# Attention with scores turned both ways: the key-major units take PV with V as weights, and their softmax totals come from Pool, a DMA turn and VectorE

## The chip, the cores and the metric

The kernel runs on one core of one Trainium2 chip. The core has a matrix engine (TensorE, PE in the profile), a vector engine (VectorE, DVE), an activation engine (ScalarE, ACT), a general engine (GpSimd, Pool or POOL) and SyncE (SP), whose queue issues most of the DMA transfers here. The metric is the device time of one execution in microseconds (us). Before the change three runs gave a median of 1304.05 us (1303.81 to 1304.19).

## The reference

A block of a transformer with modulation by a condition vector `c`: a layer norm and a modulated attention with 32 query heads over 8 cached key and value heads, and after it a gated MLP with a spatial matrix. All inputs are bf16; 2048 queries, 2048 keys, head size 128, model size 512. The attention, where the change lies, computes

```
q = (x @ wq)                         # 2048 x 512 @ 512 x 4096, 32 heads of 128
k = jnp.repeat(k_cache, 4, axis=1)   # 8 key/value heads, each shared by 4 query heads
v = jnp.repeat(v_cache, 4, axis=1)
scores = jnp.einsum('bhqd,bhkd->bhqk', q, k) * Dh ** (-0.5)
p = _softmax(scores, axis=-1)
o = jnp.einsum('bhqk,bhkd->bhqd', p, v)
attn = o.transpose(...).reshape(B, Sq, Hq * Dh) @ wo
```

The kernel takes exp(scores) without a maximum, and divides by the total of each row where it can do so late: after PV, or after the multiplication by `wo`.

## The kernel before

The attention is cut into 128 units (`NU`): unit u belongs to key/value head g = u // 16 and to the tile j = u % 16 of 128 queries, and does all 4 heads that share the key/value head: 4 x 128 queries against 2048 keys. One pass of the main loop (`for it in range(NU + 6)`, L1480) works on one unit's scores, in 8 slots. A slot issues two score matmuls (`qk`, L1006), two wide or eight narrow matmuls of P times V of an earlier unit (`pv_part`, L1474), and one matmul of the query projection (slots 0 to 3, `set_fill`) or of the multiplication by `wo` (slots 4 to 7, `wo_proj`, L1146). The order on each engine is the order in which the program issues the instructions; nothing is moved by a scheduler. `at(it, slot, fn)` (L1003) books work for a later slot.

There are two kinds of unit in the middle of the stage (`by_rows`, L982, from unit 5 on two row units and then one column unit, over and over).

- A row unit (R1 and R2 below) has queries on the partitions. ScalarE takes the exponential of 1024 scores at a time and adds up the row as it goes (`accum_out`). Then P must be turned for PV: `turn_rows` (L1075) issues one transposing DMA for each head from SP's queue, from a `pn` buffer (six of them) into the unit's `pT` buffer, and VectorE adds the two half totals and takes the reciprocal (L1082, L1085). PV (`pv_rows`, L1087) has V as weights: 16 matmuls of 128x512, one bank, one cast into `oT`. `wo_proj` then makes one matmul for each head into a bank of its own (`each`), and VectorE adds it to `xacc` scaled by the head's reciprocal (L1164).
- A column unit (C below) has keys on the partitions, so P needs no turn: ScalarE writes `pT` itself (L1065). PV (`pv`, L1106) has P as weights and V, with a column of ones, as the moving operand: 64 matmuls of 128x129, each with a weight load of its own. The column of ones gives the row totals. VectorE takes the reciprocals (L1125) and scales into `onorm` (L1126), a transposing DMA turns `onorm` into `oT` (L1137), and `wo_proj` adds up the four heads in one bank, which VectorE adds to `xacc` once (L1158).

PV of R1 comes two units later, of R2 three units later, of C one unit later (`pv_at`, with `LAGS`); so each pass has the PV of one unit, and R1's pass has that of the C before it. `wo_at` is three units after PV. Three `pT` buffers (`homes`) go round: a C unit's buffer is next written by the R2 two units later. Pool is all but idle until the last group: it clears a part of `v1` when a key/value head is loaded (L727), takes small powers for the layer norms (L683), and in the last group multiplies and adds into `x_sb` (L1187, L1188). `ln2` (L1196) and `tile_norm` (L1274) use the tiles `xn2` and `xnT2`. PSUM has two banks each for `o_ps` and `misc`, and two double banks for the scores.

Of the kernel before, what the change touches and what calls it, by code (L numbers as in the profile page):

```python
# [10 lines left out]
BF16 = mybir.dt.bfloat16  # L11
# [4 lines left out]
P = 128  # L16
# [559 lines left out]
def kernel(  # L576
# [96 lines left out]
    def bank2():  # L673
        return psum.tile([P, 1024], FP32, name="s_ps")
# [11 lines left out]
    def normalise(dst, src, mv, rstd):  # L686
        nc.vector.tensor_scalar(
            out=dst,
            in0=src,
            scalar1=mv,  # L690
            scalar2=rstd,
            op0=ALU.subtract,
            op1=ALU.mult,
        )
# [287 lines left out]
    def by_rows(u):  # L982
        return TURN_A <= u < TURN_B and (u - TURN_A) % len(LAGS) < len(LAGS) - 1

    row_units = [u for u in range(NU) if by_rows(u)]

    def pv_at(u):
# [18 lines left out]
    def qk(u, i):  # L1006
        g, j = divmod(u, NT)
        b, jj = g * NCH + j // CT, j % CT
        if i == 0:
            if homes[u] == "wsp":  # L1010
                pTs[u] = wspp.tile([P, NT, 512], BF16, name="wsp")
            else:
                pTs[u] = late.tile([P, NKT, 512], BF16, name=homes[u], bufs=1)
            if by_rows(u):
                rsums[u] = stat.tile([P, NSLOT], FP32, name="rs")
        s_ps = bank2()
        if by_rows(u):
            hh, half = divmod(i, 2)
            for c in range(2):
                k0 = (2 * half + c) * 512  # L1020
                nc.tensor.matmul(  # L1021
                    s_ps[:, c * 512 : (c + 1) * 512],
                    lhsT=qTs[b][:, hh, jj * P : (jj + 1) * P],
                    rhs=groups[g]["kT"][:, k0 : k0 + 512],
                    start=True,
                    stop=True,
                )
            nc.scalar.activation(  # L1028
                out=rows_of(u, hh)[:, half * HK : (half + 1) * HK],
                in_=s_ps[:],  # L1030
                func=ACT.Exp,
                scale=inv_sqrt_dh,
                accum_out=rsums[u][:, i : i + 1],
            )
            if half == 1:
                at(*divmod(u * NSLOT + i + 1, NSLOT), lambda: turn_rows(u, hh))
            return
        if u < 2:
            pair, k0 = i // 4, i % 4 * 4
            qs = slice(pair * 256, (pair + 1) * 256)  # L1040
            for kt in range(4):
                nc.tensor.matmul(  # L1042
                    s_ps[:, kt * 256 : (kt + 1) * 256].rearrange("p (r q) -> p r q", r=2),
                    lhsT=groups[g]["kT"][:, (k0 + kt) * P : (k0 + kt + 1) * P],
                    rhs=qTs[b][:, 2 * pair : 2 * pair + 2, jj * P : (jj + 1) * P],
                    start=(kt % 2 == 0),
                    stop=(kt % 2 == 1),
                )
            nc.scalar.activation(
                out=pTs[u][:, k0 : k0 + 4, qs],  # L1050
                in_=s_ps[:].rearrange("p (k q) -> p k q", k=4),
                func=ACT.Exp,
                scale=inv_sqrt_dh,
            )
            return
        for h in range(2):
            kt = 2 * i + h
            nc.tensor.matmul(  # L1058
                s_ps[:, h * 512 : (h + 1) * 512].rearrange("p (r q) -> p r q", r=REP),
                lhsT=groups[g]["kT"][:, kt * P : (kt + 1) * P],  # L1060
                rhs=qTs[b][:, :, jj * P : (jj + 1) * P],
                start=True,
                stop=True,
            )
        nc.scalar.activation(  # L1065
            out=pTs[u][:, 2 * i : 2 * i + 2, :],
            in_=s_ps[:].rearrange("p (k q) -> p k q", k=2),
            func=ACT.Exp,
            scale=inv_sqrt_dh,
        )  # L1070

    def rows_of(u, hh):
        return pn[(row_units.index(u) * REP + hh) % len(pn)][:, 0:SK]

    def turn_rows(u, hh):  # L1075
        c0 = u * REP + hh
        rs = rsums[u]
        nc.sync.dma_start_transpose(
            out=pTs[u][:, :, hh * P : (hh + 1) * P], in_=rows_of(u, hh)
        )  # L1080
        tot = stat.tile([P, 1], FP32, name="tot")
        nc.vector.tensor_tensor(  # L1082
            out=tot[:], in0=rs[:, 2 * hh : 2 * hh + 1], in1=rs[:, 2 * hh + 1 : 2 * hh + 2], op=ALU.add
        )
        nc.vector.reciprocal(out=rall[:, c0 : c0 + 1], in_=tot[:])  # L1085

# [58 lines left out]

    def wo_proj(u):  # L1146
        g, j = divmod(u, NT)
        each = by_rows(u)
        ps = {}

        def into(first, X_ps, scale):
            if first:
                xaccs[j] = late.tile([P, D], FP32, name=f"xacc{j}", bufs=1)
            xa = xaccs[j]
            if scale is None and first:
                nc.vector.tensor_copy(out=xa[:], in_=X_ps[:])
            elif scale is None:
                nc.vector.tensor_tensor(out=xa[:], in0=X_ps[:], in1=xa[:], op=ALU.add)  # L1158
            elif first:
                nc.vector.tensor_scalar(  # L1160
                    out=xa[:], in0=X_ps[:], scalar1=scale, scalar2=None, op0=ALU.mult
                )
            else:
                nc.vector.scalar_tensor_tensor(  # L1164
                    out=xa[:], in0=X_ps[:], scalar=scale, in1=xa[:], op0=ALU.mult, op1=ALU.add
                )

        def mm(hh):
            if hh == 0 or each:
                ps[0] = bank("misc")  # L1170
            nc.tensor.matmul(  # L1171
                ps[0][:],
                lhsT=oTs[u][:, hh, :],
                rhs=groups[g]["wo"][:, hh, :],
                start=(hh == 0 or each),
                stop=(hh == REP - 1 or each),
            )
            if each:
                c0 = u * REP + hh
                into(g == 0 and hh == 0, ps[0], rall[:, c0 : c0 + 1])  # L1180
            elif hh == REP - 1:
                into(g == 0, ps[0], None)
            if hh < REP - 1 or g < HKV - 1:
                return
            xa = xaccs[j]
            engine = nc.gpsimd if j < NT - CT else nc.vector
            engine.tensor_tensor(out=xa[:], in0=xa[:], in1=ga_rows[:], op=ALU.mult)  # L1187
            engine.tensor_tensor(  # L1188
                out=x_sb[:, j, :], in0=xa[:], in1=x_sb[:, j, :], op=ALU.add
            )  # L1190
            if j >= NT - CT:
                ln_stats(mv2, j, x_sb[:, j, :])

        return [lambda hh=hh: mm(hh) for hh in range(REP)]

    def ln2(it, j):  # L1196

        st = {}

        def first():  # L1200
            if j < NT - CT:
                ln_stats(mv2, j, x_sb[:, j, :])
            st["rstd"] = rstd_of(mv2[:, j : j + 1, :], 1, "ln2")

        def second():
            xn = res.tile([P, D], BF16, name="xn2", bufs=2)
            normalise(xn[:], x_sb[:, j, :], mv2[:, j, 0:1], st["rstd"][:, 0:1])
            st["xnT"] = res.tile([P, NDT, P], BF16, name="xnT2", bufs=2)
            nc.sync.dma_start_transpose(out=st["xnT"][:], in_=xn[:])

        def third():
            ch, c0 = j // CT, (j % CT) * P
            if ch not in h2Ts:
                h2Ts[ch] = res.tile([P, NDT, 512], BF16, name="hT", bufs=NCH)
            for dt in range(NDT):
                nc.vector.tensor_scalar(
                    out=h2Ts[ch][:, dt, c0 : c0 + P],
                    in0=st["xnT"][:, dt, :],
                    scalar1=modc[:, 4 * NDT + dt : 4 * NDT + dt + 1],
                    scalar2=modc[:, 3 * NDT + dt : 3 * NDT + dt + 1],  # L1220
                    op0=ALU.mult,
                    op1=ALU.add,
                )

        at(it + 1, 0 if j >= NT - CT else 2, first)
        at(it + 1, 4, second)
        at(it + 2, 3, third)

# [43 lines left out]
        first[j] = ln1_stats(j, 1)  # L1272

    def tile_norm(j):  # L1274
        xn = res.tile([P, D], BF16, name="xn2", bufs=2)
        normalise(xn[:], x_sb[:, j, :], mv1[:, j, 0:1], first[j][:, 0:1])
        first[j] = xn

# [193 lines left out]
        at(NU + 5, 5 + ch, lambda ch=ch: z2_norm(ch))  # L1472

    def pv_part(u, i, n):  # L1474
        if by_rows(u):
            return pv_rows(u, i, n)
        for k in range(NSLOT // n):
            pv(u, i * (NSLOT // n) + k)
# [250 lines left out]
```

## Time and profile before

| what | value |
|---|---|
| median of three runs | 1304.05 us |
| the profiled execution | 1303.83 us, of which the span is 1302.0 us |
| PE, ACT, DVE, POOL busy | 1287.0, 1112.8, 685.7, 59.0 us |
| narrow PV matmuls (L1114, 128x129) | 3200, 50 units of 64 |
| wide PV matmuls (L1093, 128x512) | 78 row units of 16 |
| transposing DMAs of P, of `onorm` | 312 and 50 |

A line of the page's fifth part, or of a table of groups, gives the line, the engine, the operation, what it writes and reads, the shape and the count, then the busy time, the mean time of one in ns, and the idle time of the engine before them. A line of a timeline gives the start and the length in us, then the same, with equal neighbours merged (x8). Lengths of matmuls overlap: what one costs is read from the start of one to the start of the next. `SPq` is the time SP's queue spends on issuing a DMA.

### The profile page before, as it was taken

How to read it: one execution, taken by the hardware profiler on the slowest of the kernel's cores; microseconds unless marked ns; L12 is line 12 of the kernel's file. 1: busy time of each engine (PE TensorE's matmuls, PEld its weight loads, DVE VectorE, ACT ScalarE, POOL GpSimd, SP SyncE). 2: the span in 40 equal slices, each digit the busy share in tenths (PEclk: the TensorE clock that was granted, in tenths of full speed). 3: DMA queues.
4: the chain of work that ended last, by engine and by line, in shares of the span. 5: the costliest groups of instructions: out<-in, count | busy, mean ns of one | idle time of the engine just before them, and what ended most of it. 6: DMA issues, size and time to landing. Idle time of an engine off the chain costs nothing.

```text
span 1302.0 us, 22572 instructions
## 1 busy us (share of the span) xinstructions
PE 1287.0 (99%) x8512; PEld 700.2 (54%) x8665; DVE 685.7 (53%) x1777; ACT 1112.8 (85%) x1683; POOL 59.0 (5%) x99
## 2 busy tenths in 40 slices
PE   9999999999999999999999999999999999999998
PEld 7655555555555555555555555555555556644445
DVE  7545455545554555455545554555455566784444
ACT  7999999999999999999999999999999998650000
POOL 2000000000000000000000000000000133410000
PEclk9999999999999999999999999999999999999999
DMA  7999999999999999999999999999999973254300
GB/s 207 183 188 181 168 184 191 190 166 188 189 181 177 186 174 189 183 171 188 190 175 181 187 192 181 169 195 173 176 193 165 172 146 91 49 138 98 81 21 32
DMA packets 774997, 211.18 MB, mean 162 GB/s; under 512 B 759264, under 2 KB 773216, under 8 KB 774880
## 3 DMA queue, kind: packets, MB, share of 16 engines
q1 hardware_dynamic: 772864, 207.94, 87.5%
q10 hardware_dynamic: 2016, 1.71, 0.4%
q8 instruction: 70, 1.15, 0.4%
q14 instruction: 47, 0.39, 0.1%
HBM read 21.37 MB, written 2.10 MB: 18 GB/s over the span
## 4 chain that ended last, share of the span: by engine, by line
PE 98%; issue 1%; ACT 1%; DMA 0%; SPq 0%; DVE 0%; ACTq 0%
PE s_ps L1021 21%; PE o_ps L1093 20%; PE o_ps L1114 14%; PE s_ps L1058 13%; PE misc L1171 8%; PE misc L959 8%; PE misc L1573 7%; PE s_ps L1397 2%; PE s_ps L1436 2%; PE o_ps L1606 1%; PE s_ps L1042 0%; PE s_ps L1606 0%; DMA kT<-in_A_k_cache_dram 0%; ACT pn L1028 0%; ACT win_sb L1028 0%
## 5 line engine op out<-in xcount | busy, mean ns | idle before, releaser
L1021 PE MATMUL s_ps<-kT,qT 128*128 128x512 bf16 x1219 | 365.0, 379 | 2.3
L1028 ACT ACTIVATE win_sb<-s_ps 128x1024 bf16<-128x1024 f32 x312 | 319.0, 1023 | 3.4 <-PE s_ps L1021 0.7
L1093 PE MATMUL o_ps<-pT,v 128*128 128x512 bf16 x909 | 272.6, 379 | 1.5
L1164 DVE SCALAR_TENSOR_TENSOR xacc<-misc,rall,xacc 128x512 f32<-128x512 f32 x304 | 227.5, 748 | 69.2 <-PE misc L1171 61.7
L1058 PE MATMUL s_ps<-qT,kT 128*128 128x512 bf16 x768 | 228.4, 379 | 0.8
L1065 ACT ACTIVATE pT<-s_ps 128x1024 bf16<-128x1024 f32 x208 | 209.8, 1024 | 11.8 <-PE s_ps L1058 3.6
L1028 ACT ACTIVATE pn<-s_ps 128x1024 bf16<-128x1024 f32 x208 | 212.7, 1023 | 2.3 <-PE s_ps L1021 0.7
L1093 PEld LDWEIGHTS <-v 128*128 128x128 bf16 x1248 | 121.9, 98 | 147.9 <-issue 1.1
L1065 ACT ACTIVATE wsp<-s_ps 128x1024 bf16<-128x1024 f32 x176 | 179.8, 1023 | 12.4 <-PE s_ps L1058 4.6
L1171 PE MATMUL misc<-wo_g,oT 128*128 128x512 bf16 x479 | 181.6, 379 | 1.0
L1021 PEld LDWEIGHTS <-qT 128*128 128x128 bf16 x1248 | 121.4, 98 | 109.4 <-issue 0.4
L959 PE MATMUL misc<-hT,wq_g 128*128 128x512 bf16 (+1 forms) x499 | 178.3, 369 | 0.5
L970 DVE CAST qT<-misc 128x512 bf16<-128x512 f32 x126 | 86.5, 687 | 153.5 <-PE misc L959 153.5
L1114 PEld LDWEIGHTS <-pT 128*128 128x128 bf16 x1792 | 119.6, 98 | 48.8
L1082 DVE TENSOR_TENSOR tot<-rs 128x1 f32<-128x1 f32 x312 | 48.4, 155 | 171.3 <-ACT win_sb L1028 114.9
L1114 PE MATMUL o_ps<-v,pT 128*128 128x129 bf16 x1792 | 137.5, 220 | 0.6
L1058 PEld LDWEIGHTS <-kT 128*128 128x128 bf16 x768 | 74.1, 98 | 81.1 <-issue 1.1
L1114 PEld LDWEIGHTS <-wsp 128*128 128x128 bf16 x1408 | 94.3, 98 | 41.5
L1114 PE MATMUL o_ps<-v,wsp 128*128 128x129 bf16 x1408 | 108.5, 220 | 0.5
L1028 ACT ACTIVATE wmod_a<-s_ps 128x1024 bf16<-128x1024 f32 x104 | 106.3, 1023 | 0.6 <-PE s_ps L1021 0.4
L1573 PE MATMUL misc<-wsp,z 128*128 128x512 bf16 (+2 forms) x554 | 100.1, 336 | 0.3
L1093 PE MATMUL o_ps<-wsp,v 128*128 128x512 bf16 x292 | 87.8, 379 | 0.4
(118 smaller groups left out, 894.6 us busy)
## 6 DMA issues: line engine op xcount, KB each, us to landing
wo_g<-in_A_wo_dram SPq DMA_DIRECT2D x8, 512.0 KB, 4.5
wq_g<-in_A_wq_dram SPq DMA_DIRECT2D x7, 512.0 KB, 4.1
v<-in_A_v_cache_dram SPq DMA_DIRECT2D x7, 512.0 KB, 4.7
wsp<-in_w_mod_dram SPq DMA_DIRECT2D x1, 2048.0 KB, 9.1
pT<-win_sb SPq DMA_TRANSPOSE x117, 5.0
win_sb<-in_B_w_in_dram SPq DMA_DIRECT2D x1, 1792.0 KB, 7.3
x_sb<-in_A_x_dram SPq DMA_DIRECT2D x3, 512.0 KB, 7.0
out_dram<-yout ACTq DMA_DIRECT2D x12, 128.0 KB, 1.7
```

Source lines behind the costliest of these rows:

```text
L959: nc.tensor.matmul(ps[0][:, o0 : o0 + n], lhsT=wqs[g][:, dt, hh * DH : (hh + 1) * DH], rhs=hTs[ch][:, dt, c0 : c0 + n], start=(dt == 0), s ...
L970: nc.vector.tensor_copy(out=dst, in_=src)
L1021: nc.tensor.matmul(s_ps[:, c * 512 : (c + 1) * 512], lhsT=qTs[b][:, hh, jj * P : (jj + 1) * P], rhs=groups[g]["kT"][:, k0 : k0 + 512], sta ...
L1028: nc.scalar.activation(out=rows_of(u, hh)[:, half * HK : (half + 1) * HK], in_=s_ps[:], func=ACT.Exp, scale=inv_sqrt_dh, accum_out=rsums[u ...
L1058: nc.tensor.matmul(s_ps[:, h * 512 : (h + 1) * 512].rearrange("p (r q) -> p r q", r=REP), lhsT=groups[g]["kT"][:, kt * P : (kt + 1) * P], ...
L1065: nc.scalar.activation(out=pTs[u][:, 2 * i : 2 * i + 2, :], in_=s_ps[:].rearrange("p (k q) -> p k q", k=2), func=ACT.Exp, scale=inv_sqrt_dh,)
L1082: nc.vector.tensor_tensor(out=tot[:], in0=rs[:, 2 * hh : 2 * hh + 1], in1=rs[:, 2 * hh + 1 : 2 * hh + 2], op=ALU.add)
L1093: nc.tensor.matmul(o_pss[u][:], lhsT=groups[g]["v1"][:, kt, 0:DH], rhs=pTs[u][:, kt, :], start=(kt == 0), stop=(kt == NKT - 1),)
L1114: nc.tensor.matmul(o_ps[:, hh % 2, 0 : DH + 1], lhsT=pTs[u][:, kt, hh * P : (hh + 1) * P], rhs=groups[g]["v1"][:, kt, 0 : DH + 1], start=( ...
L1164: nc.vector.scalar_tensor_tensor(out=xa[:], in0=X_ps[:], scalar=scale, in1=xa[:], op0=ALU.mult, op1=ALU.add)
L1171: nc.tensor.matmul(ps[0][:], lhsT=oTs[u][:, hh, :], rhs=groups[g]["wo"][:, hh, :], start=(hh == 0 or each), stop=(hh == REP - 1 or each),)
L1573: nc.tensor.matmul(g_pss[f][:, :n], lhsT=z2[:, st, f * P : (f + 1) * P], rhs=wsp[t][:, st, c0 : c0 + n], start=(st == 0), stop=(st == NT - ...
```

## The change

The 35 column units from 7 to 109 (`by_sums`) take PV in the row units' way, with V as weights, and multiply by `wo` one head at a time, scaled by the reciprocals. As their P has keys on the partitions and the column of ones is no longer used, their totals are made anew in `key_sums`: Pool adds the 16 key tiles of P into one tile `acc` of 128 x 512 (15 adds, the last one into a bf16 tile `sums`); two units later SP turns the 128 x 512 `sums` by DMA into a buffer of `xn1`; one unit after that VectorE sums 128 values for each of the four heads, and takes the reciprocals. The turn of `onorm` falls away for these units. The adding of the two half totals of a row unit becomes a `tensor_reduce` over the pair instead of a `tensor_tensor` of its two halves. `xn2` and `xnT2` give way to the one tile `acc`, which serves both.

```diff
+    def by_sums(u):
+        return TURN_A <= u < (HKV - 1) * NT and not by_rows(u)
...
+            if by_sums(u):
+                key_sums(u)
...
+    def key_sums(u):
+        acc = res.tile([P, D], FP32, name="acc", bufs=2)
+        sums = late.tile([P, REP, DH], BF16, name="onorm", bufs=3)[:].rearrange(
+            "p r q -> p (r q)"
+        )
+        pT = pTs[u]
+
+        def add(kt):
+            nc.gpsimd.tensor_tensor(
+                out=acc[:] if kt < NKT - 1 else sums,
+                in0=pT[:, 0, :] if kt == 1 else acc[:],
+                in1=pT[:, kt, :],
+                op=ALU.add,
+            )
+
+        for kt in range(1, NKT):
+            at(*divmod(u * NSLOT + kt // 2 + 1, NSLOT), lambda kt=kt: add(kt))
+
+        turned = {}
+
+        def turn():
+            xn = res.tile([P, D], BF16, name="xn1", bufs=4)
+            turned["t"] = xn[:].rearrange("p (r q) -> p r q", r=REP)
+            nc.sync.dma_start_transpose(out=turned["t"], in_=sums)
+
+        def close():
+            tot = stat.tile([P, REP], FP32, name="tot4")
+            nc.vector.tensor_reduce(out=tot[:], in_=turned["t"], axis=AX.X, op=ALU.add)
+            nc.vector.reciprocal(out=rall[:, u * REP : (u + 1) * REP], in_=tot[:])
+
+        at(u + 2, 3, turn)
+        at(u + 3, 2, close)
...
         tot = stat.tile([P, 1], FP32, name="tot")
-        nc.vector.tensor_tensor(
-            out=tot[:], in0=rs[:, 2 * hh : 2 * hh + 1], in1=rs[:, 2 * hh + 1 : 2 * hh + 2], op=ALU.add
+        nc.vector.tensor_reduce(
+            out=tot[:], in_=rs[:, 2 * hh : 2 * hh + 2], axis=AX.X, op=ALU.add
         )
...
     def wo_proj(u):
         g, j = divmod(u, NT)
-        each = by_rows(u)
+        each = by_rows(u) or by_sums(u)
...
-            xn = res.tile([P, D], BF16, name="xn2", bufs=2)
-            normalise(xn[:], x_sb[:, j, :], mv2[:, j, 0:1], st["rstd"][:, 0:1])
-            st["xnT"] = res.tile([P, NDT, P], BF16, name="xnT2", bufs=2)
-            nc.sync.dma_start_transpose(out=st["xnT"][:], in_=xn[:])
+            both = res.tile([P, D], FP32, name="acc", bufs=2)[:].bitcast(BF16)
+            xn = both[:, 0:D]
+            normalise(xn, x_sb[:, j, :], mv2[:, j, 0:1], st["rstd"][:, 0:1])
+            st["xnT"] = both[:, D : 2 * D].rearrange("p (d q) -> p d q", d=NDT)
+            nc.sync.dma_start_transpose(out=st["xnT"], in_=xn)
...
     def pv_part(u, i, n):
-        if by_rows(u):
+        if by_rows(u) or by_sums(u):
             return pv_rows(u, i, n)
```

More of the change, by code (lines that the diff above doesn't have):

```diff
@@ L1274, in tile_norm @@
     def tile_norm(j):
-        xn = res.tile([P, D], BF16, name="xn2", bufs=2)
+        xn = res.tile([P, D], FP32, name="acc", bufs=2)[:].bitcast(BF16)[:, 0:D]
         normalise(xn[:], x_sb[:, j, :], mv1[:, j, 0:1], first[j][:, 0:1])
```

## The prediction

> **What bounds the kernel now.** I read the page first, then the table of waits of PE alone, then the timeline of PE over one period of units, and last the stretches where Pool already works beside VectorE, and SP's queue. The page:
>
> ```profile
> span 1302.0 us, 22572 instructions
> PE 1287.0 (99%) x8512; PEld 700.2 (54%) x8665; DVE 685.7 (53%) x1777; ACT 1112.8 (85%) x1683; POOL 59.0 (5%) x99
> PEclk9999999999999999999999999999999999999999
> PE 98%; issue 1%; ACT 1%; DMA 0%; SPq 0%; DVE 0%; ACTq 0%
> ```
>
> PE is busy from end to end, at full granted clock, and is 98% of the chain. The waits of PE add up to under 2 us, all in the first 30 us. So only less PE time makes this kernel faster, and a new wait costs time only once it reaches PE. The PE timeline, in units (C is a column unit, R1 and R2 the row units after it):
>
> ```profile
> 509.56 0.59 PE L1058 MATMUL s_ps<-qT,kT 128*128 128x512 bf16 x2
> 509.99 0.59 PE L1093 MATMUL o_ps<-pT,v 128*128 128x512 bf16 x2
> 510.42 0.38 PE L959 MATMUL misc<-hT,wq_g 128*128 128x512 bf16 x1
> 510.64 0.59 PE L1058 MATMUL s_ps<-qT,kT 128*128 128x512 bf16 x2
> ...
> 518.19 0.59 PE L1021 MATMUL s_ps<-kT,qT 128*128 128x512 bf16 x2
> 518.62 0.62 PE L1114 MATMUL o_ps<-v,pT 128*128 128x129 bf16 x8
> 519.08 0.38 PE L959 MATMUL misc<-hT,wq_g 128*128 128x512 bf16 x1
> 519.29 0.38 PE L1021 MATMUL s_ps<-kT,qT 128*128 128x512 bf16 x1
> ...
> 527.00 0.59 PE L1021 MATMUL s_ps<-kT,qT 128*128 128x512 bf16 x2
> ```
>
> C runs from 509.56 to 518.19 (8.63 us), with a wide PV (two 128x512 a slot); R1 from 518.19 to 527.00 (8.81 us), with the narrow PV of C (eight 128x129). The R2 before (500.93 to 509.56) works its scores by rows with a wide PV and takes 8.63 us. So the narrow PV alone makes R1 longer: 8.81 - 8.63, and over all starts (period 26.073, C 8.633, R1+R2 17.44) it is 17.44 - 2 x 8.633 = 0.174 us.
>
> **The change on PE.** by_sums holds for units 7, 10, ... 109: 35 units. Each swaps 64 narrow matmuls and 64 weight loads for 16 wide ones; the matmuls of W_o stay four. 35 x 0.174 = 6.1 us. R1 then has R2's mix of instructions, which holds 8.63 us today, so no other engine sets R1's pace sooner: ACT's row exponentials started every 0.99 to 1.01 us between 51.5 and 55.5 us, where PE had less to do, against PE's 1.079 a slot. What is left to show is that nothing new reaches PE.
>
> **VectorE.** Per C unit it loses two reciprocals (169 ns), two onorm products (424) and one add (681), 1.87 us, and gains one oT cast (691), four scaled adds (748), one tensor_reduce of 128x512 and a reciprocal (164). The nearest reduce is the single 128x512 row of 686 ns in the last stage: 4.5 us in all. 13.09 us busy of 26.07 become 15.8 of 25.9 (61%). C's four scaled adds fall into the R1 behind the next C, one bank each, as R2's own do in an R2 today without a wait of PE: cost nothing; the cover is the second misc bank.
>
> **Pool** gets 15 chained adds of 128x512 a unit; today it has none there. The nearest rows are its two adds and products of the last stage, shown where VectorE works beside it:
>
> ```profile
> 1048.96 1.27 POOL L1187 TENSOR_TENSOR xacc<-xacc,ga_rows 128x512 f32<-128x512 f32 x1 [4.30 <-DVE xacc L1158]
> 1049.08 0.17 DVE L1125 RECIPROCAL rall<-o_ps 128x2 f32<-128x2 f32 x1 [0.20 <-PE o_ps L1114]
> 1049.28 0.42 DVE L1126 TENSOR_TENSOR onorm<-o_ps,rall 128x256 bf16<-128x256 f32 x1
> 1049.85 0.40 DVE L1082 TENSOR_TENSOR tot<-rs 128x1 f32<-128x1 f32 x1
> 1050.28 0.16 DVE L1085 RECIPROCAL rall<-tot 128x1 f32<-128x1 f32 x1
> 1050.31 1.16 POOL L1188 TENSOR_TENSOR x_sb<-xacc,x_sb 128x512 bf16<-128x512 f32 x1
> 1050.37 0.75 DVE L1164 SCALAR_TENSOR_TENSOR xacc<-misc,rall,xacc 128x512 f32<-128x512 f32 x1
> ```
>
> The pair starts 1.35 us apart though the second needs the first (gap 0.08). An add with one bf16 input lies between 1.15 and 1.28; bounds for the pitch of the chain are 1.15 (shortest row, no gap) and 1.45 (longest row 1.37 plus the gap). I take 1.28, nearest to the second row (f32 and bf16 in) with its gap. The first add waits for C's first exponential, 1.75 us into C (ACT's ends at 511.21). Pool's other work there, a memset of v1 in six of the C units, stands ahead of a chain while Pool is idle: nothing. So the sum is ready E = 1.75 + 15 x 1.28 = 21 us after C's start (19 to 23.5).
>
> Who waits for E? First SP: R2 takes C's pT buffer, so its first row transpose waits until Pool has read it, and SP's queue behind it. That queue today, in the next R1 and R2 (C started at 509.56):
>
> ```profile
> 529.04 2.31 SPq L1078 DMA_TRANSPOSE pT<-wmod_a  x1
> 531.43 1.52 SPq L1137 DMA_TRANSPOSE oT<-onorm  x1
> 533.05 4.55 SPq L1078 DMA_TRANSPOSE pT<-pn  x2
> 537.70 5.07 SPq L1078 DMA_TRANSPOSE pT<-win_sb  x2
> 542.82 2.82 SPq L744 DMA_TRANSPOSE kT<-in_A_k_cache_dram  x1
> ```
>
> SP is behind here: R2's first transpose could start at 529.8 and starts at 533.05. Without C's oT turn ahead of it, SP comes to it 21.7 us after C's start, so an E of 21 holds nothing and one of 23.5 holds SP for 1.8 us. The turn of the sums goes behind that transpose: same size and number as the 35 oT turns that go, so DMA carries no more. R2's PV comes 26 us after R2's start, 10 us after its last transpose is issued; its first pn buffer is written again some 18 us after its transpose starts; the next R1 needs SP at 547.1, 4.4 us after the last of R2's (1.5 us after a kT load). The wait costs nothing at 21, and nothing or tenths in seven periods at 23.5.
>
> Second VectorE: the sums' turn is issued at 21.7 + 2.2 = 23.9 and lands 2.8 us later, at 26.7, 0.8 us into the next C. VectorE reaches the reduce in slot 2 of that C and has nothing to do from 1.6 to 4.5 us into it (idle 2.92 us before the qT cast), so the 0.85 us of reduce and reciprocal fit; behind them are that cast and the W_o adds. The result is wanted in the R1 after it. Cost nothing. Cover ends when E + 2.2 + 2.8 + 0.85 passes the cast's time, 25.9 + 4.5: E = 24.5, a pitch of 1.52; PE waits for the cast's bank about 1 us later, from a pitch of 1.58.
>
> **Totals of rows.** In the stretch above tot, with both inputs in SBUF, takes 0.40 instead of 0.15 us and ends when Pool's product ends (1050.25 and 1050.23); reciprocal and scaled add (one SBUF tensor) are not held, nor is Pool. The edit makes tot a one-input reduce. I price it at the same 0.15 us, by the reciprocal beside it. The Trainium skill, SBUF — State Buffer, section "Who interferes with whom", says that a VectorE instruction with two SBUF inputs contends with a GpSimd instruction that reads SBUF, and that tensor_reduce on trn2 never does; the trace agrees on the first (0.15 to 0.40), and no run here shows the second. The same section says that one-input copies and scalar operations may take the shared ports too, which would speak against 15 Pool adds a period; the casts here read PSUM and kept 0.69 us beside Pool at 1040.27. By that page the sum stays 6.1; if a reduce is held as tot is, it is the second rival.
>
> The merged acc tile replaces xn2 and xnT2 with as many buffers: nothing. **Sum:** 1303.83 (profiled, span 1302.0) - 6.1 = 1297.7; the median is 0.2 above the profiled run, so 1298.0.
>
> **Rivals.** *Slower: the chain of adds is the bound.* Its place is VectorE's reduce, waiting in front of the qT cast. Above 1.58 us each 0.1 us of pitch costs 1.5 us a period, 52 us in all; it eats the gain at 1.59. At 1.7, 35 x 1.8 = 63 us less 6: 1361. For it: 15 adds in place, 74% busy beside VectorE, is a load that no stretch shows. Against: 24 rows of 1.15 to 1.37 us, unmoved by VectorE.
>
> *A one-input total is held too.* A hold is up to 1.28 us, on 74% of eight totals a period. A W_o bank is wanted again 1.9 us after it is written and the scaled add takes 0.75, which leaves about 1.0 us less the reciprocal: some 20% of holds pass it, by 0.15 us on average, for the four totals inside W_o: 0.1 us a period, 3 to 4 us. 1301 to 1302. Against: the held row alone has two SBUF inputs.
>
> *Small losses*: SP held 1 to 2 us at a slower pitch, with R1's transposes after a load landing late (its last is issued at 529.04 and lands 4.7 us later by the median, 2.3 us before its PV at 536.06): up to 1 us in the seven or fourteen periods with loads, or part of the 0.174 staying. 1299 to 1301.
>
> *No gain*: ACT or VectorE paces R1 at 8.8 whatever PV does: 1304. R2 with the same mix at 8.63 speaks against it.
>
> **Chances.** Forecast (1297 to 1299) 0.66; small losses 0.10, held totals 0.05; no gain 0.04; slower by the chain or a wait that I don't see, 0.15. A measurement of this kernel tells about 0.2% (2.6 us) from no change. Faster: the forecast, small losses and most of held totals, 0.79; same: no gain and the rest, 0.06; slower 0.15. The range from 1296.8 (a shade over the full gain) to 1301.6 takes in small losses and half of the held totals, and leaves out about 0.2.
>
> **What would show it.** Right: R1 at 8.63 us in PE's timeline and no wait of PE; o_ps 128x129 matmuls down from 3200 to 960; Pool adds 1.2 to 1.35 us apart, the last ending before 22 us; the 128x512 reduce near 0.69 us inside VectorE's idle time in C; tot near 0.15 without rows of 0.4. Wrong: PE waiting for a cast or a scaled add in C or R1, or for a transpose at a row PV; VectorE waiting long for the turned sums; Pool adds above 1.5 us apart.

## The result and the profile after

Six runs of the changed kernel gave a median of 1297.71 us (1297.41 to 1297.81), six of the kernel before beside them 1303.93 us (1303.74 to 1304.19). The ratio is 0.9952, with an interval of 0.9939 to 0.9965: 6.2 us faster. The forecast was 1298.0, from 1296.8 to 1301.6. The profiled execution took 1297.41 us.

The page of the changed kernel, with the lines that answer to those of before, the busiest line of Pool and the line of the row totals:

```profile
span 1295.6 us, 20137 instructions
PE 1281.8 (99%) x6860; PEld 628.2 (48%) x6985; DVE 775.1 (60%) x1847; ACT 1109.0 (86%) x1683; POOL 665.2 (51%) x624
PEclk9999999999999999999999999999999999999999
PE 98%; issue 1%; ACT 1%; DMA 0%; SPq 0%; DVE 0%; ACTq 0%
...
L1085 POOL TENSOR_TENSOR acc<-acc,wsp 128x512 f32<-128x512 f32 x234 | 270.5, 1156 | 18.3
...
L1120 DVE TENSOR_REDUCE tot<-rs 128x1 f32<-128x2 f32 x312 | 46.1, 148 | 115.0 <-ACT win_sb L1033 76.3
```

PE is still 98% of the chain at full granted clock. Pool went from 59 to 665 us busy and VectorE from 686 to 775; Pool isn't in the chain at all, and VectorE stays at 0%. The PE timeline over one period, in the same three units as before (C, R1, R2, and the C after them):

```profile
506.32 0.59 PE L1063 MATMUL s_ps<-qT,kT 128*128 128x512 bf16 x2
506.75 0.59 PE L1131 MATMUL o_ps<-pT,v 128*128 128x512 bf16 x2
...
514.95 0.59 PE L1026 MATMUL s_ps<-kT,qT 128*128 128x512 bf16 x2
515.38 0.59 PE L1131 MATMUL o_ps<-pT,v 128*128 128x512 bf16 x2
...
523.58 0.59 PE L1026 MATMUL s_ps<-kT,qT 128*128 128x512 bf16 x2
...
532.22 0.59 PE L1063 MATMUL s_ps<-qT,kT 128*128 128x512 bf16 x2
```

The starts are 8.63, 8.63 and 8.64 us apart, 25.90 in all. R1, which took 8.81 us with the narrow PV, now has two 128x512 matmuls in each slot like the others, and takes as long as they do. The waits of PE over the whole run (waiting tile and line, what ended the wait, then us in total, times, longest):

```profile
PE o_ps L778 <- DVE onorm L769: 1.2, 1, 1.2
PE misc L898 <- DVE xn L687: 0.6, 1, 0.6
PE o_ps L857 <- DMA kT<-in_A_k_cache_dram: 0.3, 1, 0.3
```

All three belong to the stages ahead of the pattern. Nothing that the change added reaches PE. Pool's timeline from the C that starts at 506.32:

```profile
508.11 1.15 POOL L1085 TENSOR_TENSOR acc<-pT 128x512 f32<-128x512 bf16 x1 [7.47 <-ACT pT L1070]
509.34 15.97 POOL L1085 TENSOR_TENSOR acc<-acc,pT 128x512 f32<-128x512 f32 x13
525.39 1.16 POOL L1085 TENSOR_TENSOR onorm<-acc,pT 128x512 bf16<-128x512 f32 x1
534.01 1.15 POOL L1085 TENSOR_TENSOR acc<-wsp 128x512 f32<-128x512 bf16 x1 [7.47 <-ACT wsp L1070]
```

The first add starts 1.79 us into C and the last ends 20.2 us into it. From the first start to the last are 17.28 us, 14 steps of 1.234. Then Pool stands idle for 7.47 us until the next C. SP's queue issues the turn of these sums:

```profile
527.46 2.45 SPq L1116 DMA_TRANSPOSE pT<-pn  x1
530.00 1.34 SPq L1100 DMA_TRANSPOSE xn<-onorm  x1
531.43 1.85 SPq L1116 DMA_TRANSPOSE pT<-pn  x1
```

SP comes to R2's first transpose at 527.46, 21.1 us after C's start. Pool had let go of the buffer 0.9 us earlier, so SP isn't held. VectorE in the next C, which starts at 532.22:

```profile
533.73 0.67 DVE L1104 TENSOR_REDUCE tot<-xn 128x4 f32<-128x512 bf16 x1
534.43 0.18 DVE L1105 RECIPROCAL rall<-tot 128x4 f32<-128x4 f32 x1
536.73 0.69 DVE L970 CAST qT<-misc 128x512 bf16<-128x512 f32 x1 [2.13 <-PE misc L959]
```

Reduce and reciprocal lie in the gap ahead of the qT cast, and 2.13 us of the gap are left. In VectorE's table of waits the turned sums came late in 6 of 35 units, 1.6 us at most, which the gap takes:

```profile
DVE tot L1104 <- DMA xn<-onorm: 5.2, 6, 1.6
```

### The profile page after: what moved, and what is told of

The parts are those of the page before. It is cut to its first block, busy times and chain, and to the rows that moved or that the text cites. A ratio compares the mean times of both kernels' runs of the same rounds, so it can differ in the third digit from the quotient of the medians.

```text
span 1295.6 us, 20137 instructions
## 1 busy us (share of the span) xinstructions
PE 1281.8 (99%) x6860; PEld 628.2 (48%) x6985; DVE 775.1 (60%) x1847; ACT 1109.0 (86%) x1683; POOL 665.2 (51%) x624
## 4 chain that ended last, share of the span: by engine, by line
PE 98%; issue 1%; ACT 1%; DMA 0%; SPq 0%; DVE 0%; ACTq 0%
PE o_ps L1131 30%; PE s_ps L1026 21%; PE s_ps L1063 13%; PE misc L1209 8%; PE misc L959 8%; PE misc L1612 7%; PE o_ps L1152 4%; PE s_ps L1436 2%; PE s_ps L1475 2%; PE o_ps L1645 1%; PE s_ps L1047 0%; ACT pn L1033 0%; PE s_ps L1645 0%; DMA kT<-in_A_k_cache_dram 0%; ACT pT L1054 0%
## 5 line engine op out<-in xcount | busy, mean ns | idle before, releaser
L1202 DVE SCALAR_TENSOR_TENSOR xacc<-misc,rall,xacc 128x512 f32<-128x512 f32 x441 | 330.3, 749 | 86.5 <-PE misc L1209 72.7
L1131 PE MATMUL o_ps<-pT,v 128*128 128x512 bf16 x1157 | 348.3, 379 | 3.1
L1131 PEld LDWEIGHTS <-v 128*128 128x128 bf16 x1808 | 176.9, 98 | 213.3
L1085 POOL TENSOR_TENSOR acc<-acc,wsp 128x512 f32<-128x512 f32 x234 | 270.5, 1156 | 18.3
L1085 POOL TENSOR_TENSOR acc<-acc,pT 128x512 f32<-128x512 f32 x221 | 255.5, 1156 | 17.3
L959 PE MATMUL misc<-hT,wq_g 128*128 128x512 bf16 (+1 forms) x523 | 187.4, 369 | 0.2
L1131 PE MATMUL o_ps<-wsp,v 128*128 128x512 bf16 x563 | 169.8, 379 | 1.5
L1120 DVE TENSOR_REDUCE tot<-rs 128x1 f32<-128x2 f32 x312 | 46.1, 148 | 115.0 <-ACT win_sb L1033 76.3
L1085 POOL TENSOR_TENSOR acc<-wsp 128x512 f32<-128x512 bf16 x18 | 20.7, 1151 | 149.9 <-ACT wsp L1070 149.9
L1140 DVE CAST oT<-o_ps 128x512 bf16<-128x512 f32 x113 | 78.2, 692 | 16.7 <-PE o_ps L1131 4.6
```

What stands on the lines that cost most here:

```text
L959: nc.tensor.matmul(ps[0][:, o0 : o0 + n], lhsT=wqs[g][:, dt, hh * DH : (hh + 1) * DH], rhs=hTs[ch][:, dt, c0 : c0 + n], start=(dt == 0), s ...
L1085: nc.gpsimd.tensor_tensor(out=acc[:] if kt < NKT - 1 else sums, in0=pT[:, 0, :] if kt == 1 else acc[:], in1=pT[:, kt, :], op=ALU.add,)
L1131: nc.tensor.matmul(o_pss[u][:], lhsT=groups[g]["v1"][:, kt, 0:DH], rhs=pTs[u][:, kt, :], start=(kt == 0), stop=(kt == NKT - 1),)
L1140: nc.vector.tensor_copy(out=oTs[u][:], in_=o_pss[u][:].rearrange("p (r q) -> p r q", r=REP))
L1202: nc.vector.scalar_tensor_tensor(out=xa[:], in0=X_ps[:], scalar=scale, in1=xa[:], op0=ALU.mult, op1=ALU.add)
```

## The experiments

The prediction left three things to be settled: whether the whole gain is PE's and the new work costs nothing, what the edit of the row totals is worth, and how far Pool's chain of adds is from costing time. The runs below are changes to the changed kernel; ratios are to the kernel before.

**No totals at all (`pe_alone`).**

```diff
+    nc.gpsimd.memset(rall[:], 1.0 / SK)
...
-            if by_sums(u):
-                key_sums(u)
```

> The wide PV and the four scaled adds stay; Pool's adds, the turn of the sums, the reduce and its reciprocal are left out for the 35 units, and their factors are a constant (1/2048) written once at the start, so that the totals of these units are not computed. Theory (the whole chain of Pool, SP and VectorE is hidden, the gain is PE's alone): 1297.7 us within 0.3. Rival (the chain is hidden only in part: SP's queue or VectorE passes some of it on): faster than the changed kernel by 0.5 to 3 us, 1294.7 to 1297.2.

Measured: 1297.56 us (1297.27 to 1297.65), ratio 0.9948 [0.9934, 0.9962].

```profile
PE 1289.1 (99%) x6985; PEld 628.5 (49%) x6985; DVE 747.4 (58%) x1777; ACT 1107.9 (86%) x1683; POOL 59.7 (5%) x100
```

Without the 525 adds, 35 turns and 35 reduces the kernel is 0.15 us faster, less than the 0.4 us by which the runs of either kernel differ. The gain is PE's alone, and the new work is hidden to within some 0.2 us.

**Units by sums only up to 60 (`half`)**, 18 units instead of 35.

```diff
-        return TURN_A <= u < (HKV - 1) * NT and not by_rows(u)
+        return TURN_A <= u < 60 and not by_rows(u)
```

> The change for the first 18 of the 35 units only. Theory (0.18 us for each unit, nothing shared): 1304.0 - 18 x 0.18 = 1300.8. Rival (a part of the gain comes from something that the change does once): 1298 to 1300 or 1301.5 to 1303.

Measured: 1300.78 us (1300.35 to 1302.55), ratio 0.9977 [0.9968, 0.9986]. By PE's starts a period is 25.90 us long up to 532 us, where the pass with the PV of the last such unit is over, and 26.07 after it. Of 6.2 us, 3.15 are there with 18 of 35 units (3.2 by proportion). The gain is a sum over units, not the removal of one late place.

**The row totals back to two inputs (`tot_two`).**

```diff
-        nc.vector.tensor_reduce(
-            out=tot[:], in_=rs[:, 2 * hh : 2 * hh + 2], axis=AX.X, op=ALU.add
+        nc.vector.tensor_tensor(
+            out=tot[:], in0=rs[:, 2 * hh : 2 * hh + 1], in1=rs[:, 2 * hh + 1 : 2 * hh + 2], op=ALU.add
```

> The changed kernel with the row units' total as an add of two inputs again. Theory by the prediction's second rival (an add with two inputs in SBUF is held until Pool's add ends, up to 1.2 us, on 71% of eight totals a period, and some of the holds pass the slack of a bank of W_o): 3 to 4 us slower, 1301 to 1302, with tot rows up to 1.3 us and a mean near 0.6. Rival (VectorE's slack takes the holds): 1297.7, with the same long tot rows. Second rival (no hold outside the few rows of before): 1297.7 with tot at 0.15.

Measured: 1297.65 us (1297.4 to 1298.06), ratio 0.9949 [0.9935, 0.9962]: no change. All the totals of this kernel as one group (ns at least, median and at most; first and last start), and one of them beside Pool's timeline:

```profile
L1120 DVE TENSOR_TENSOR tot<-rs x312: 126/160/799, 53.0 to 1052.8; 128x1 f32<-128x1 f32 x156
```

```profile
522.04 2.39 POOL L1085 TENSOR_TENSOR acc<-acc,pT 128x512 f32<-128x512 f32 x2
...
522.67 0.54 DVE L1120 TENSOR_TENSOR tot<-rs 128x1 f32<-128x1 f32 x1
```

This total starts at 522.67 inside Pool's first add and is done at 523.21, when that add is (half of the 2.39 us, to 523.2). Of the 312 totals 177 start while Pool works, 174 of them inside a chain; 114 of the 177 take more than 0.2 us, 0.34 on average over the 177 against 0.15 outside, and 0.80 at most. Each of the 114 ends 14 to 21 ns after a Pool instruction does. So the hold is real, and it costs nothing: the table of waits shows no wait of PE for it. With one input, in the changed kernel, the same 312 take 122 to 156 ns, inside the chains and out. This is what the Trainium skill states (SBUF — State Buffer, section "Who interferes with whom"): instructions of VectorE with two SBUF inputs contend with GpSimd's reads, tensor_reduce does not. The trace now shows both halves, and that the edit buys no time here.

**A longer chain (`chain17`, `chain19`, `chain21`).** Pool adds `pT[:, 0, :]` to the sum and takes it away again, once, twice or three times ahead of its last add.

```diff
+        def again(op):
+            nc.gpsimd.tensor_tensor(out=acc[:], in0=acc[:], in1=pT[:, 0, :], op=op)
...
+            if kt == NKT - 1:
+                for _ in range(2):
+                    at(u + 1, 0, lambda: again(ALU.add))
+                    at(u + 1, 0, lambda: again(ALU.subtract))
```

(`range(2)` is `chain19`; 1 and 3 are the others.)

> Two more Pool instructions in each chain (the first key tile added and subtracted again ahead of the last add). At the measured pitch of 1.235 us the sum is ready 22.7 us after C's start instead of 20.2. Theory (VectorE's cast is the first to feel it, from 24.5 us, PE from 25.5): no change, 1297.7. Rival (SP gives first: R2's first transpose is held 1.6 us longer than SP's own lateness, and R1's transposes behind a load come late): 0.3 to 1 us slower, with PE waiting at R1's PV.

> Four more Pool instructions in each chain; the sum is ready at 25.2 us. Theory (the limit is VectorE in front of the qT cast, PE waits from 25.5): 1297.7 to 1300, VectorE waiting for the turned sums in every period. Rival (SP's queue is the limit: R2's first transpose held 4 us, which is all the time SP has to spare in a period): 1308 to 1318, with PE waiting for transposes at a row PV, and worst after loads.

> Six more Pool instructions in each chain; the sum is ready 27.6 us after C's start. Theory (as the run with four more showed in its worst periods: VectorE's reduce waits for the turned sums, the qT cast behind it is late, PE waits for its bank; the limit is near 25 us): every period is longer by 27.6 - 25.2 = 2.4 us, 35 x 2.4 = 84 us over the run with four more, 1380 to 1395. Rival (Pool's own load is the limit: 21 x 1.235 = 25.9 us is just one period, and VectorE's wait is made good): 1306 to 1315.

| kernel | chain ends, us after C's start | time, us | over the changed kernel | ratio to before |
|---|---|---|---|---|
| changed | 20.24 | 1297.71 | | 0.9952 [0.9939, 0.9965] |
| `chain17` | 22.70 | 1297.96 (1297.48 to 1299.15) | 0.25 | 0.9953 [0.9938, 0.9969] |
| `chain19` | 25.17 | 1305.67 (1304.75 to 1305.93) | 8.0 | 1.0011 [1.0001, 1.002] |
| `chain21` | 27.69 | 1342.33 (1341.6 to 1344.15) | 44.6 | 1.03 [1.0284, 1.0315] |

`chain17` uses up cover and no time: VectorE waits for the turned sums in 21 units, 24.2 us in all, and PE never for that. At 25.2 us the cover begins to fail. Lines of `chain19`, PE's waits first, then VectorE's, then the time from issue to landing of the 35 turns of the sums:

```profile
PE misc L1216 <- DVE qT L970: 2.0, 5, 0.6
PE misc L1216 <- DVE xacc L1209: 1.3, 1, 1.3
...
PE misc L1305 <- DVE xn L1295: 1.2, 2, 0.8
```

```profile
DVE tot L1111 <- DMA xn<-onorm: 101.8, 35, 3.9
```

```profile
DMA to landing us min/median/max: 2.5/3.5/5.0
```

One of these places, in a C that starts at 431.32, from VectorE and from PE:

```profile
436.73 0.69 DVE L1111 TENSOR_REDUCE tot<-xn 128x4 f32<-128x512 bf16 x1 [3.82 <-DMA xn<-onorm]
437.45 0.18 DVE L1112 RECIPROCAL rall<-tot 128x4 f32<-128x4 f32 x1
437.54 0.66 DVE L970 CAST qT<-misc 128x512 bf16<-128x512 f32 x1
```

```profile
438.26 0.38 PE L1216 MATMUL misc<-wo_g,oT 128*128 128x512 bf16 x1 [0.52 <-DVE qT L970]
```

VectorE stands 3.82 us in front of the reduce, the cast behind it is late, and PE waits 0.52 us for the bank that the cast empties, in slot 5 of C. That is the place that the prediction gave. By PE's starts, 4.4 of the 8.0 us are spread over twelve periods that are 0.1 to 0.7 us longer than 25.90; the table lists only the five longest of these waits. Two single places make up most of the rest with about 1.5 us each. One is at 984 us, where a scaled add stands behind the reduce of the last unit, which waits 3.25 us for its sums. The other is a unit at 89 us in which the modulation's VectorE instruction `xn` L1295 was held (the last section).

The chain ends at 25.1 to 25.4 us in all 35 units; what sets the costly ones apart is the landing of the turn. In the 13 units ahead of the twelve periods and of the place at 984 us it took 3.6 to 5.0 us from issue to landing, in the 22 others 2.5 to 3.57. So it is a late landing that breaks the cover first; what delayed these landings isn't shown. VectorE's reduce starts 4.8 us after the next C's start or later where PE then loses 0.1 us or more, and at 4.2 us in most of the others, which so have some 0.6 us left: by these numbers, an estimate, PE would feel every unit from a chain end of about 25.7 us.

`chain21` turns it into a standing wait, 27 times instead of 5:

```profile
PE misc L1216 <- DVE qT L970: 30.1, 27, 2.3
```

But 44.6 us over 35 periods are 1.27 us a period, where 2.4 was expected, and 2.0 by the estimate above for a chain that ends 27.7 us after C's start. The starts of C tell why: early in the run they alternate, 27.2, 26.5, 27.3, 26.5 us apart, and later 27.6, 26.1, 27.6, 26.1. PE's wait comes in slot 5 of a C whose own chain already runs, so the delay gives that chain's turn and reduce as much more time, and the next period is delayed by less. Two neighbouring delays add up to 1.9 to 2.0 us: a delay d is followed by one of about 2.0 - d, 1.0 a period on average, half of the overrun. The rest of the 1.27 lies in single passes, most of all in one of 30.0 us, in which PE's clock fell (the last section).

**The same long chain, its reduce later (`chain21_late`).** As `chain21`, and VectorE's reduce is booked behind the cast, in the first R1 slots after it:

```diff
-        at(u + 3, 2, close)
+        at(*((u + 4, 1) if u + 4 < NU - NT else (u + 3, 2)), close)
```

> The chains of 21 Pool instructions again, but VectorE's reduce and reciprocal move from slot 2 of the next C to slot 1 of the R1 behind it, past the qT cast and the scaled adds that they held up (the last unit's stay). Theory (what cost 44.6 us was the place of the reduce in VectorE's order, and neither Pool's load of 25.9 us a period nor SP held by 6 us): 1297.7 to 1302. Rival (Pool's load or SP's lateness passes on to PE by itself): 1310 to 1342, with PE waiting for transposes at a row PV.

Measured: 1326.82 us (1324.75 to 1327.94), ratio 1.0174 [1.0159, 1.019]. 15.5 of the 44.6 us come back, so VectorE's place in front of the cast was a cause, but not the only one. PE's waits:

```profile
PE o_ps L1138 <- DMA pT<-pn: 11.5, 7, 2.5
PE o_ps L1138 <- DMA pT<-win_sb: 4.7, 6, 1.4
PE misc L1216 <- DVE xacc L1209: 2.6, 1, 2.6
PE o_ps L1138 <- issue: 2.4, 2, 1.2
PE o_ps L1138 <- DMA pT<-wmod_a: 1.3, 3, 0.5
```

The waits for the cast are gone, and in their place PE waits at a wide PV for a row unit's transposes (`pT<-pn`; the other names are tiles that share those buffers). The chain now ends 27.6 to 30.2 us after C's start, SP can't turn R2's P before that (by the table of waits of its queue SP waits 29 times for Pool's adds, 138.8 us in all), and everything behind it in SP's queue is late, up to R1's transposes. The waits in the table add up to some 22 us of the 29 still lost; the rest I have not placed.

**The adds on VectorE (`sums_vector`).**

```diff
-            nc.gpsimd.tensor_tensor(
+            nc.vector.tensor_tensor(
```

> The 15 adds go to VectorE, all else as in the changed kernel. Theory (VectorE has no room for them: 15 x 0.69 us, the row of its f32 add in the last stage, on 60% of 25.9 us is 26 us, and in C's pass alone 4.4 + 10.4 us of work in 8.6 us, so casts and scaled adds come late and PE waits): 3 to 6 us a period, 1400 to 1510. Rival (the adds are faster there than on Pool and VectorE has 40% to spare): 1298 to 1305.

Measured: 1404.72 us (1404.57 to 1404.82), ratio 1.0773 [1.0757, 1.079].

```profile
PE 1303.6 (93%) x6860; PEld 627.0 (45%) x6985; DVE 1091.7 (78%) x2372; ACT 1108.6 (79%) x1683; POOL 59.0 (4%) x99
```

```profile
PE misc L1209 <- DVE xacc L1202: 47.7, 64, 0.8
PE misc L959 <- DVE xacc L1202: 25.4, 34, 0.8
PE misc L1209 <- DVE qT L970: 9.3, 34, 0.6
```

VectorE has 9 us more to do in a period and still 22% of the span idle, yet the period grows by 3.15 us to 29.05: the adds stand in its queue in front of casts and scaled adds that PE waits for. For this kernel that weighs against a rule of thumb of the Trainium skill (GPSIMD Engine Reference, section "Engine selection"), which gives elementwise additions to VectorE as the faster engine. An add is faster there (0.69 us by the median against 1.156), and the kernel 107 us slower.

**More units by sums (`until112`, `until121`).** The bound of `by_sums` is moved by one column unit (112) or by four, to all column units (112, 115, 118, 121).

```diff
-        return TURN_A <= u < (HKV - 1) * NT and not by_rows(u)
+        return TURN_A <= u < TURN_B and not by_rows(u)
```

(`until121`; in `until112` the bound is `u <= (HKV - 1) * NT`.)

> The change for the four column units of the last group as well (112, 115, 118, 121). Theory (PE gains 4 x 0.18 us, but Pool also has the products and adds of the last group, 2.4 us a unit, behind the chain, and VectorE waits for x_sb): between 0.7 us faster and 3 us slower than the changed kernel, 1297.0 to 1300.7, with VectorE's statistics waiting longer for Pool. Rival (Pool's last group is hidden too): 1297.0.

> The change for one unit more, 112, whose chain ends before Pool's first product of the last group. Theory: 0.18 us faster than the changed kernel, 1297.5. Rival (the chain meets Pool's work or the loads of the last group): 1298 to 1303.

`until112` took 1297.66 us (1297.45 to 1299.13), ratio 0.9953 [0.9939, 0.9966], not to be told from the changed kernel. `until121` took 1318.36 us (1318.02 to 1318.8), ratio 1.0111 [1.0095, 1.0126], 20.7 us more, far outside what was expected. PE's waits and VectorE's:

```profile
PE misc L1209 <- DVE xacc L1202: 14.4, 3, 7.5
```

```profile
DVE bnst L698 <- POOL x_sb L1226: 25.1, 8, 9.4
```

The last group is where Pool has work of its own, and the timeline shows what the chain does to it (Pool, VectorE, PE):

```profile
1030.49 12.38 POOL L1085 TENSOR_TENSOR acc<-acc,pT 128x512 f32<-128x512 f32 x10
...
1042.83 1.26 POOL L1225 TENSOR_TENSOR xacc<-xacc,ga_rows 128x512 f32<-128x512 f32 x1
1044.17 1.15 POOL L1226 TENSOR_TENSOR x_sb<-xacc,x_sb 128x512 bf16<-128x512 f32 x1
...
1045.35 0.69 DVE L698 BATCH_NORM_STATS2 bnst<-x_sb 128x6 f32<-128x512 bf16 x1 [6.94 <-POOL x_sb L1226]
...
1047.20 0.58 PE L1209 MATMUL misc<-wo_g,oT 128*128 128x512 bf16 x1 [5.26 <-DVE xacc L1202]
```

Pool's product stands behind the first eleven adds of the chain; VectorE waits 6.94 us for it, with the scaled adds of W_o behind; PE waits 5.26 us for the bank of one of them. Three such waits, of 1.6, 5.3 and 7.5 us, are 14.4 us. For the rest there is the granted clock (after the counts of PE, PEld, DVE, ACT and POOL: PEclk, DMA share, GB/s):

```profile
1046.00:1052.00 6.00, 4.80 (x12) 1.72 (x12) 2.62 (x10) 2.23 (x4) 4.67 (x6) 0.50 0.00 0
...
1080.00:1089.00 9.00, 4.50 (x11) 1.70 (x12) 4.99 (x10) 2.05 (x2) 8.01 (x9) 0.50 0.00 1
```

PE stands still in the two long waits from 1041.9 to 1047.2 us and from 1076.8 to 1084.3. The clock is still 1.00 from 1042 to 1045 and from 1077 to 1079; then it is 0.50, and 1.00 again from 1053 and from 1090. So it fell while PE was waiting, some 3 us into each wait, and the matmuls behind the wait started 0.43 us apart where 0.22 is usual. PE worked some 10.5 us at half the clock, which loses about 5.3 us; with the waits that is 19.7 of the 20.7 us. That the waits lower the clock is read from this order of time; no run tests it by itself.

No version beats the changed kernel by more than its runs scatter.

## Why the prediction was right, and where it was off

- **PE's gain**: 35 units by 0.174 us, 6.1, against 6.2 measured. By the starts it is 26.073 - 25.900 = 0.173 a period, 6.06 in all. The remaining 0.1 to 0.2 us aren't placed: the trace before has a pause of 0.22 us in a pass at 92.17 us that the trace after doesn't have, but the trace after has a period of 26.63 us from 972.5 us on where before has 26.43; what either waited for isn't shown.
- **R1 at R2's pace**: right, 8.63 us. The rival that ACT would hold R1 at 8.8 fell: ACT was busy 8.72 of R1's 8.81 us before and 8.56 of 8.63 after, with 16 instructions in both, so its busy time followed PE.
- **Nothing new reaches PE**: right, shown by the table of waits and by `pe_alone` (0.15 us, inside the scatter).
- **Pool's chain**: the mechanism was right, the pitch mis-sized: 1.234 against 1.28 (bounds 1.15 to 1.45). An add with one bf16 input took 1.156 us and the gap 0.07 to 0.08. Over 35 chains the end came 20.24 us after C's start, not 21.
- **SP and the turn**: R2's first transpose came at 21.1 for 21.7, the turn at 24.0 on average for 23.9, and landed 2.8 us later by the median, as priced.
- **VectorE**: 15.64 us a period against 15.8; the 128x512 reduce took 667 to 687 ns against 686. It lay in the gap named, with 2.1 us to spare where it came on time.
- **The totals with one input**: priced at 0.15 us, measured 0.148. But the rival that a held total would cost 3 to 4 us was over-priced: `tot_two` holds 114 totals, up to 0.80 us, and costs nothing. The step that failed is the share of holds, 20%, that was to pass the bank's slack of 1.0 us less the reciprocal (0.16): the longest hold was some 0.65 us (0.80 less 0.15), where up to 1.28 was allowed for, and by the trace none reached PE.
- **The limit of the cover**: put at a chain end of 25.5 us for PE. The place, the reduce in front of the qT cast, was right. The limit has a term that was mis-sized: the turn's landing was taken at its median, 2.8 us, for every unit. `chain17` at 22.7 costs nothing, but `chain19` at 25.2, still inside the limit, costs 8 us, nearly all of it behind turns that landed after 3.6 to 5.0 us and behind the one held instruction. For the units that land early about 25.7 comes out of `chain19`, close to the forecast.
- **The price beyond the limit**: wrong by a factor of two. The prediction let each late microsecond count in every period (1.5 us for 0.1 us of pitch). In `chain21` two neighbouring delays together make up the 2.0 us of overrun, because the delay falls in a pass whose own chain runs already. At the pitch of 1.7 that the slower rival named, the loss would by the same halving, an estimate, have been nearer half of 63 us.
- **SP held by the chain**: counted at nothing or tenths. Right for this chain. `chain21_late` shows it as the second limit, close behind the first and hidden by it.

## What to carry to other kernels

Where PE is 98% of the chain, the time of the kernel is PE's starts, one to the next: moving 64 narrow matmuls to 16 wide ones was worth what the difference of two neighbouring units said, to a tenth of a microsecond over the whole run. An idle engine can take a long serial chain for nothing as long as its end, with the slowest landing of a DMA behind it, comes before the place in another engine's queue where its result is waited for; that place, and not the sum of busy times, sets the limit, as 5 us more of chain and the same adds on an engine that is 60% busy show. Before such a chain is put on an engine, look at every stretch of the program where that engine has other work: four more units cost 20.7 us where 35 had cost nothing.

## What was not expected of the hardware

- A one-input instruction of VectorE, with both ends in SBUF, was held beside Pool's adds. In `chain19` the product of `ident` (bf16, 128x128) with a column took 243 to 244 ns five times of eight, and 0.48, 0.89 and 1.15 us while Pool's longer chain ran beside it; the two longest end at 92.10 and 90.87 us, Pool's adds at 92.05 and 90.82. In the changed kernel, where that chain ends earlier, the eight take 235 to 251 ns. PE waited 1.2 us for it:

```profile
L1295 DVE TENSOR_SCALAR xn<-ident,modc x8: 243/244/1148, 89.2 to 92.3; 128x128 bf16<-128x128 bf16 x8
```

  The Trainium skill (SBUF — State Buffer, section "Who interferes with whom") states that one-input copies and scalar operations may take the shared ports too; this place agrees. The 128x512 casts from PSUM kept 0.66 to 0.69 us beside Pool.
- A held instruction of VectorE came free when the Pool instruction that it met ended: 14 to 21 ns after it for all 114 held totals of `tot_two`, and 0.05 us after it for the two longest `xn` above. So no hold was longer than one add of 1.16 us; the longest total took 0.80 us.
- A chain that comes too late costs less than its overrun, if what it delays is itself the start of the next period's deadline: periods of 27.6 and 26.1 us in turn, where 25.9 is usual.
- The granted clock fell to half during waits of PE of 5.3 and 7.5 us in `until121`, and stayed there for some 7 and 10 us. In `chain21` it fell once, 0.9 us after a wait of 2.27 us had ended, and the line shows that stretch; 26 other waits for the same cast, up to 2.2 us, and waits of 2.5 and 2.6 us in `chain21_late` brought no such fall. So a wait of 2 to 3 us can cost more than its length, and these runs don't show what decides it.

```profile
563.50:566.50 3.00, 3.00 (x9) 1.06 (x7) 1.59 (x3) 1.88 (x2) 2.84 (x3) 0.50 1.15 214
```
